# Backward convolution in descending order, Q turned ahead through scratch, weight pieces turned by one DMA each

## The chip, the cores and the metric

The kernel runs on one core of one Trainium2 chip. The metric is the device time of one execution in microseconds; three runs of the kernel before took 1823.18, 1831.09 and 1841.0 us (median 1831.09). Engines are named as in the profile: PE (TensorE), DVE (VectorE), ACT (ScalarE), POOL (GpSimd) and SP (SyncE). SP does no arithmetic; it issues DMAs, in order. Each engine works through its own instructions in order, and what another engine or a DMA has to deliver first is waited for.

## The reference, cut to what matters

One forward pass of a gated block and all its gradients: x + s * g, where s is a state-space convolution over 2048 positions and g a gated feed-forward layer. Sizes: L = 2048, D = 576, N = 128, F = 4608, all inputs bfloat16.

```python
def _fwd_reference(...):
    xn = _layernorm(A_u, axis=-1)
    # s: K[d, l] = Re sum_n C P(d, n, l) dB, P = exp(dt A l); y = conv(xn, K) + xn * Dskip
    s = _A_ref(xn, A_re, A_im, B_re, B_im, C_re, C_im, log_dt, Dskip)
    # g: silu( (silu(xn w1) * (xn w3)) w2 )
    g = _silu(_B_ref(xn, w1, w3, w2))
    return A_u + s * g

def reference(...):
    _out, _vjp = jax.vjp(_f, A_u, A_re, ..., Dskip, w1, w3, w2)
    return (_out, *_vjp(grad_out))     # the output and 12 gradients
```

## The kernel before, in words

The forward part (to about 720 us) makes the convolution kernel and its spectra, the feed-forward layer's hidden values and the output. On its way it writes to DRAM what the backward part needs: `Q_dram` (36 chunks of 128 x 2048, factors of P for 16 channels each), `PZ_dram`, the spectra `UH_dram`, `KH2_dram` and `KHz_dram`, and the hidden values `U_dram`, `G_dram`, `H_dram`.

The last stage of the forward part, `ffn_output`, makes the 16 output tiles of 128 positions. Each needs a block `hc` of H, turned by a DMA from DRAM into one of three buffers, and sums into one of three PSUM pools (psA, psB, psC, by i % 3). `finish` then computes the output and its gradients on ACT and DVE; its product `e` is the last reader of the tile's PSUM. The first loads of the backward part are issued on SP among these.

The backward part (`backward`, T0 = 700) runs 18 groups of 256 hidden columns. In each, PE makes `ph` from `w2T` and `goT`, DVE multiplies it into `gu_n` and `gg_n`, both are stored to `GU_dram` and `GG_dram` by SP, and PE makes the weight gradients from them and from `h_n` (`pgw`). `w2T` is turned by a DMA from rows of w2 in SBUF.

Beside groups 0 to 10 runs the backward convolution, in four quarters of 144 channels (`conv_bwd_quarter`). A quarter turns the incoming gradient into four spectra G (`dft_folded`), then has two halves: the first multiplies G with the spectra of u (`UH_dram`, tiles `A2`, `Az`), for i from 3 down to 0, and gives the gradient of the kernel (`gK_dram`); the second multiplies G with the kernel's spectra (`KH2_dram`, `KHz_dram`, in the same tiles) and gives the gradient of xn (`gx`, stored to `GXN_dram`). Output block i (or j) needs the spectra 0 to 3 - i, and G from i to 3. Each product is `cmul_acc`, five DVE instructions. `spectrum_variants` makes the second copy of a spectrum that `cmul_acc` reads.

From group 11 on, the gradients of the parameters are summed chunk by chunk, in 72 halves (`param_step`). `param_loads` fetches a chunk two ahead: Q's chunk, turned by a DMA from DRAM into `qT`, two pieces of `gK_dram` into `gz`, and `pz`. `param_half` then has 8 small matmuls (into `et_ps`), and DVE multiplies (`pr_q`) and sums (`S_all`).

After the groups, `phase6_inputs` makes the gradient of xn in 16 tiles: 72 steps of two matmuls each (`px`), the left side from `GG_dram` and `GU_dram`, turned by DMAs into `acts`, the right side from the turned weights w1 and w3. 26 of the 72 weight blocks (`wA`) are turned during groups 14 to 17; the other 46 come in 8 pieces of 7 or 2 blocks of 128 hidden columns, into buffers that the groups leave. `load_piece` turns a piece by five DMAs, one for each 128 (the last 64) rows of the weight. `phase5_*` finishes the parameter gradients from the sums, first turning `exp(log_dt)` into columns on PE.

What sets the order: every instruction has a priority, set by `at(us)` to a planned time, and the program is ordered per engine once, before it runs, by these and by data. `issue_after` (and `Chain`) put one instruction behind another. From group 11 on (`self.chain`), SP's DMAs keep the order of the text (`sp`). Pools with `bufs=n` make the next use of a buffer wait for the readers of the one n before. All DMA turns are issued by SP through `nat_transpose` (L1631 of the kernel before).

Of the kernel before, what the change touches and what calls it, by code (L numbers as in the profile page):

```python
# [17 lines left out]
P = 128  # L18
# [68 lines left out]
class K:  # L87
# [759 lines left out]
    def cmul_acc(self, acc, A2, Az, B, tp, first, conj):  # L847
        nc, KT = self.nc, self.cfg.KT
        Q, Wq = acc.shape[1], acc.shape[4]
        tt_ = nc.vector.tensor_tensor  # L850
        f = lambda t_: t_[:].rearrange("p q r k d -> p q r (k d)")
        if first:
            tt_(out=f(acc), in0=f(A2), in1=f(B), op=ALU.mult)
        else:
            t1 = tp.tile([P, Q, 2, KT, Wq], BF16, name="cm_t")
            tt_(out=f(t1), in0=f(A2), in1=f(B), op=ALU.mult)
            tt_(out=f(acc), in0=f(acc), in1=f(t1), op=ALU.add)
        t2 = tp.tile([P, Q, 2, KT, Wq], BF16, name="cm_t")
# [3 lines left out]
        tt_(out=f(acc)[:, :, 1], in0=f(acc)[:, :, 1], in1=f(t2)[:, :, 1], op=ALU.subtract if conj else ALU.add)  # L862

# [177 lines left out]
    def ffn_output(self, T0, TB):  # L1041
# [9 lines left out]
        with self.pool(name="o_gap", bufs=1) as gap, \  # L1051
# [38 lines left out]
            def begin(i):  # L1090
# [77 lines left out]
    def ssm_bwd_conv(self, T0, TQ, ps):  # L1168
# [3 lines left out]
        with self.pool(name="b_g", bufs=1, side="right") as self.bgp, \  # L1172
                self.pool(name="b_k", bufs=1, side="right") as kp, self.pool(name="b_z", bufs=2, side="right") as zp:
            self.at(T0)
# [52 lines left out]
    def conv_bwd_quarter(self, g, kp, zp, ps, T0, TQ):  # L1227
# [23 lines left out]
        G = []  # L1251
        first = self.pe_last
# [14 lines left out]
        if g:  # L1267
            self.at(T0)
            fold(slice(0, NB))
        for b in range(NB):  # L1270
            self.at(T0 + (TQ * 0.05 * b if g else 0))
            after = None
            if g == 0 and b == NB - 1:
# [4 lines left out]
                after = self.pe_last  # L1278
            G.append(self.bgp.tile([P, 1, 2, KT, W], BF16, name=f"g_{b}"))
            if g == 0:  # L1280
# [43 lines left out]
        for b in range(NB):  # L1324
            A2[b] = kp.tile([P, 1, 2, KT, W], BF16, name=f"a2_{b}")
            Az[b] = kp.tile([P, 1, KT, W], BF16, name=f"az_{b}")
            nc.sync.dma_start(out=A2[b][:, 0], in_=self.KH2_dram[g, b])
            nc.sync.dma_start(out=Az[b][:, 0], in_=self.KHz_dram[g, b])
        for j in range(NB):
            self.at(T0 + TQ * (0.6 + 0.1 * j))  # L1330
# [6 lines left out]
            ev = zp.tile([P, 2, W], FP32, name="gev")  # L1337
# [36 lines left out]
    def phase5_open(self, pool):  # L1374
# [3 lines left out]
        NB = self.NB  # L1378
        lr = pool.tile([NB, P], BF16, name="lg_b", tag="gh6")
        st = self.small.tile([P, 3 * NB + 3], FP32, name="sm_b")  # L1380
# [5 lines left out]
        for row, vec in self.block_rows(lr, self.aps["A_log_dt"]):  # L1386
            nc.gpsimd.dma_start(out=row, in_=vec)
        self.er = er = pool.tile([NB, P], FP32, name="er_b", tag="gh6")
        nc.scalar.activation(out=er[:], in_=lr[:], func=ACT.Exp)

    def phase5_turn(self):
        nc, NB, er = self.nc, self.NB, self.er
        pt = self.ps_T.tile([P, 512], FP32, name="et_ps")
        with self.tc.issue_after(self.pe_last.ins):
            nc.tensor.transpose(pt[:, 0:NB], er[:], self.ident_f[0:NB, 0:NB])
        nc.vector.tensor_copy(out=self.dtb[:, 0], in_=pt[:, 0:NB])
        nc.vector.tensor_tensor(out=self.dtb[:, 1], in0=self.dtb[:, 0], in1=self.dtb[:, 0], op=ALU.mult)
# [88 lines left out]
    def backward(self, T0, TG, TQ, TC, TX, gctx, mats):  # L1486
# [12 lines left out]
        with ExitStack() as out:  # L1499
# [40 lines left out]
            self.params_open(S_all, ps)  # L1540
            step = self.param_step
            hs = {}
            for gi in range(NG):
# [9 lines left out]
                for stage in group if gi == 0 else self.phase6_group(gi, cur, elp, gwp, ps_h, ps_gw):  # L1553
# [4 lines left out]
                    if stage in ("h1", "h3"):  # L1558
                        if gi < NG - 1:
                            w2(gi, stage == "h3")  # L1560
                        elif stage == "h3":
                            self.phase5_open(elp)
                        if stage == "h3" and gi + 2 < NG:
# [424 lines left out]
```

## Time and profile before

| what | us |
|---|---|
| three runs, median | 1831.09 |
| three runs, lowest and highest | 1823.18, 1841.0 |
| the profiled execution | 1837.89 |
| its span, first to last instruction | 1836.1 |
| PE busy (matmuls) | 1672.5 |
| DVE busy | 1359.4 |
| ACT busy | 912.7 |
| POOL busy | 345.2 |

The stages by the trace: forward to about 722 us; groups 0 to 10 with the backward convolution to 1206; groups 11 to 17 (parameters beside them) to 1485; the gradient of xn to the end. The groups end at 786.6, 828.2, 866.4, 908.7, 955.7, 993.1, 1039.9, 1084.4, 1125.1, 1168.7, 1205.8, 1240.5, 1277.0, 1315.2, 1353.9, 1402.8, 1439.6 and 1484.6 us.

How to read it: a line of instructions gives start, duration, engine, line of the kernel, operation, and out<-in; `x15` means that many in a row. A line of waits says who waited for whom, the total in us, how often, and the longest. SP's own instructions (SPq) are the issue of DMAs: their length is the time for which SP is held, and the data land later. All turned loads of one kind (DMA_TRANSPOSE), by the trace:

```
L1631 SPq DMA_TRANSPOSE wT<-in_B_w_dram x40: 1227/1266/3711, 1426.4 to 1530.4; - x40
L1631 SPq DMA_TRANSPOSE w2T<-w2r x36: 1200/1270/6878, 596.9 to 1380.6; - x36
L1631 SPq DMA_TRANSPOSE qT<-Q_dram x36: 1727/2520/10050, 1188.5 to 1772.2; - x36
L1631 SPq DMA_TRANSPOSE acts<-GG_dram x16: 4850/5568/13779, 1479.2 to 1782.0; - x16
L1631 SPq DMA_TRANSPOSE wA<-in_B_w_dram x10: 1425/1787/8957, 1242.9 to 1407.1; - x10
```

(least, median and longest time that one holds SP in ns, then the first and last start in us).

### The profile page before, as it was taken

What the parts mean: (1) busy time and instruction counts of PE and PEld (TensorE: products, weight loads), DVE (VectorE), ACT (ScalarE), POOL (GpSimd) and SP (SyncE); (2) the same over time, 40 slices, a digit from 0 to 9 for tenths busy, and PEclk for the clock granted to TensorE, in tenths of its full rate; (3) what the DMA queues carried; (4) which work ended last, traced back from release to release, by engine and by line L of the source; (5) the groups of instructions that cost most, each with busy time, mean ns of one, the idle gap of its engine ahead of it and who ended that gap; (6) DMA issues with size and microseconds to landing.
All of it is one profiled execution on the core that took longest, in us unless ns stands there. A gap on an engine that the chain in (4) does not pass through costs nothing. (4 is left out here: it accounts for less than half of the span.)

```text
span 1836.1 us, 38742 instructions
## 1 busy us (share of the span) xinstructions
PE 1672.5 (91%) x15573; PEld 1236.7 (67%) x15637; DVE 1359.4 (74%) x2103; ACT 912.7 (50%) x1648; POOL 345.2 (19%) x565
## 2 busy tenths in 40 slices
PE   7789999999999899799999999999979885989997
PEld 3455555554546677687788787888868774768875
DVE  7768888795864555874975979669979935867675
ACT  6778888877762112755656667554535310000101
POOL 3112222123142110011111111111111233131132
PEclk9999999999999999899999999999989997999999
DMA  7889999779799995477664656689998999999992
GB/s 223 275 270 346 316 345 313 279 262 283 236 271 231 216 212 153 167 216 207 184 196 149 197 171 190 178 254 263 229 218 221 193 224 212 217 214 232 216 254 49
DMA packets 636506, 416.91 MB, mean 227 GB/s; under 512 B 425430, under 2 KB 576966, under 8 KB 631718
## 3 DMA queue, kind: packets, MB, share of 16 engines
q1 hardware_dynamic: 580644, 287.34, 63.2%
q0 software_dynamic: 31904, 106.81, 18.1%
q10 hardware_dynamic: 23778, 20.28, 4.0%
q8 instruction: 122, 2.00, 0.5%
q14 instruction: 58, 0.48, 0.1%
HBM read 135.60 MB, written 190.89 MB: 178 GB/s over the span
## 5 line engine op out<-in xcount | busy, mean ns | idle before, releaser
L1809 PEld LDWEIGHTS <-acts 128*128 128x128 bf16 x2304 | 226.6, 99 | 84.0 <-DMA acts<-GU_dram 9.3
L1759 PEld LDWEIGHTS <-xn_bf 128*128 128x128 bf16 x2304 | 225.2, 98 | 44.1 <-issue 17.2
L1809 PE MATMUL px<-wT,acts 128*128 128x288 bf16 x1472 | 196.0, 291 | 11.5 <-DMA wT<-in_B_w_dram 11.5
L1368 DVE TENSOR_TENSOR pr_q<-et_ps,pz 128x1024 f32<-128x1024 f32 x144 | 175.9, 1221 | 31.2 <-PE et_ps L1363 23.2
L1699 PE MATMUL ph<-w2T,goT 128*128 128x256 bf16 x1440 | 177.2, 278 | 13.2 <-ACT gh L1702 9.7
L1010 PEld LDWEIGHTS <-xnT 128*128 128x128 bf16 x1152 | 107.0, 98 | 108.5 <-issue 17.5
L1371 DVE TENSOR_REDUCE S_all<-pr_q 128x32 f32<-128x1024 f32 x144 | 175.2, 1217 | 3.1
L1699 PEld LDWEIGHTS <-goT 128*128 128x128 bf16 x1440 | 142.0, 100 | 33.7 <-issue 11.3
L1010 PE MATMUL pu<-wmB_w,xnT 128*128 128x512 bf16 x568 | 152.9, 379 | 0.5 <-issue 0.2
L1739 PE MATMUL pgw<-go_o,h_n 128*128 128x288 bf16 x1152 | 150.2, 288 | 3.4 <-DVE h_n L1677 2.7
L1010 PE MATMUL pg<-wmB_w,xnT 128*128 128x512 bf16 x526 | 143.6, 379 | 7.8 <-issue 5.2
L1759 PE MATMUL pgw<-gu_n,xn_bf 128*128 128x256 bf16 x1152 | 136.7, 275 | 9.3 <-ACT gw L1743 5.2
L1739 PEld LDWEIGHTS <-h_n 128*128 128x128 bf16 x1152 | 113.2, 99 | 32.1 <-DVE h_n L1677 3.0
L1759 PE MATMUL pgw<-gg_n,xn_bf 128*128 128x256 bf16 x1152 | 130.3, 272 | 3.0 <-ACT gw L1761 2.9
L1761 ACT CAST gw<-pgw 128x256 bf16<-128x256 f32 x144 | 52.2, 374 | 146.0 <-PE pgw L1759 146.0
L1024 ACT ACTIVATE s_t<-pg 128x512 bf16<-128x512 f32 x144 | 87.8, 610 | 72.2 <-PE pu L1018 38.1
L1809 PE MATMUL px<-wA,acts 128*128 128x288 bf16 x832 | 110.6, 289 | 11.9 <-DMA acts<-GU_dram 8.7
L1702 ACT CAST gh<-ph 128x512 bf16<-128x512 f32 x144 | 82.1, 603 | 75.7 <-PE ph L1699 60.4
L660 ACT ACTIVATE cs_k<-et_ps 128x512 bf16<-128x512 int16 x216 | 111.5, 632 | 0.9 <-PE et_ps L658 0.9
L1038 POOL DMA_DIRECT2D G_dram<-g_t x72 | 52.2, 725 | 288.6 <-DVE g_t L1028 146.1
L1865 ACT ACTIVATE go<-gx 128x576 bf16<-128x576 f32 x16 | 10.9, 683 | 191.8 <-DVE gx L1848 111.5
L1029 ACT CAST u_t<-pu 128x512 bf16<-128x512 f32 x144 | 87.5, 608 | 8.4 <-PE pu L1010 7.4
(317 smaller groups left out, 3208.2 us busy)
## 6 DMA issues: line engine op xcount, KB each, us to landing
U_dram<-u_t POOLq DMA_DIRECT2D x72, 256.0 KB, 5.5
G_dram<-g_t POOLq DMA_DIRECT2D x72, 256.0 KB, 4.9
H_dram<-h_t SPq DMA_DIRECT2D x72, 256.0 KB, 3.9
Q_dram<-q_k SPq DMA_DIRECT2D x36, 512.0 KB, 5.0
h_n<-U_dram POOLq DMA_DIRECT2D x18, 1024.0 KB, 8.5
gg_n<-G_dram POOLq DMA_DIRECT2D x18, 1024.0 KB, 7.1
GU_dram<-gu_n SPq DMA_DIRECT2D x36, 512.0 KB, 4.7
GG_dram<-gg_n SPq DMA_DIRECT2D x36, 512.0 KB, 10.6
```

What stands on the lines that cost most here:

```text
L660: self.sin_last = nc.scalar.activation(out=CS[:, :, o:o + 256], in_=pt[:].bitcast(I16)[:, :, 0::2], func=ACT.Sin, scale=6.283184 / 2 ** 16)
L1010: ins = nc.tensor.matmul(pt[:], lhsT=xnT[:, c, ts], rhs=wm[w][:, c, :], start=(q == 0 and c == 0), stop=(q == 1 and c == nfull - 1))
L1024: nc.scalar.activation(out=s_t[:, :, q, :], in_=pgv, func=ACT.Silu)
L1029: nc.scalar.copy(out=u_t[:, :, q, :], in_=puv)
L1038: self.u_stores[step] = nc.gpsimd.dma_start(out=dst[fb * ng:(fb + 1) * ng, :, i0:i0 + NT, :].rearrange("g p t f -> p g (t f)"), in_=src[:] ...
L1368: nc.vector.tensor_tensor(out=pr[:].rearrange("p r k e -> p r (k e)"), in0=T[h][:].rearrange("p k z d a -> p (k z d a)")[:, None].to_broad ...
L1371: nc.vector.tensor_reduce(out=self.S_all[:, :, d0:d0 + 4], in_=pr[:].rearrange("p r k (d a) -> p (r k) d a", d=4), op=ALU.add, axis=AX.X)
L1699: self.pe_last = nc.tensor.matmul(ph[j][:, k, :].rearrange("p (a f) -> p a f", f=P), lhsT=lw, rhs=rh, start=(n == 0), stop=(n == nfull))
L1702: self.sc(lambda: nc.scalar.copy(out=gh[:, j], in_=ph[j][:]))
L1739: self.pe_last = nc.tensor.matmul(pgw[pi_][:, 0:pw], lhsT=hn[:, tt, fl * P:(fl + 1) * P], rhs=go_o[:, tt, po:po + pw], start=(tt == 0), st ...
L1759: self.pe_last = nc.tensor.matmul(pw_[:, 0:FG], lhsT=self.xn_bf[:, tt, c * P:(c + 1) * P], rhs=nat[:, tt, :], start=(tt == 0), stop=(tt == ...
L1809: self.pe_last = nc.tensor.matmul(px[pi_][:, 0:pw], lhsT=acts[i][:, ai, fi, :], rhs=w[:, po:po + pw], start=(n == 0), stop=(n == len(steps ...
```

## The change

1. **Q turned ahead.** `turn_q(n, after)` turns n chunks, each in two halves: a DMA turn of 128 x 1024 into one of two buffers, and a plain store of it to a new scratch `QT_dram`. All are chained on SP: turn 0, turn 1, store 0, turn 2, store 1, and so on. It is called in the backward convolution, behind the spectra's loads: 3 chunks beside the second half of quarter 0, 3 and 3 beside quarters 1 and 2, 3 and 6 beside quarter 3: 24. The next half's spectra are loaded behind the last store (`q_last`). `param_loads` then fetches chunks 0 to 23 by one plain DMA of 512 KB; chunks 24 to 35 are turned as before.
2. **Descending second halves.** The second half runs j from 3 to 0, and its last block takes its products in the order 0, 3, 1, 2. In quarters 1 to 3, G is made from 3 down to 0, the first half is planned from 0.1 of the quarter, and `spectrum_variants` is made for one spectrum at a time, just ahead of its first use. `gx` and its partner `gev` move from a pool of two buffers to one of one.
3. **One DMA per weight piece** in `load_piece`: 576 rows at once.
4. **log_dt.** `phase5_open` is called ahead of the groups, and not in the last one; the vector is turned on PE as it is, and the exponential is taken by ACT from PSUM afterwards.
5. **At the end of the forward part**: the last output tile sums in psC instead of psA; the rows of w2 are first loaded behind hc 7 (was 4), and the first turns of w2T stand behind hc 13.

```diff
@@ ffn_output
-                return i, hc, x_t, go_t, s_t, (psA, psB, psC)[i % 3].tile([P, 2, 512], FP32, name="po")
+                return i, hc, x_t, go_t, s_t, (psA, psB, psC)[i % 3 if i < LT - 1 else 2].tile([P, 2, 512], FP32, name="po")
@@ ssm_bwd_conv
+            self.turnp, self.turned_q, self.q_last = turnp, 0, None
+            self.QT_dram = self.dram.tile([cfg.D // 16, P, 16 * cfg.N], BF16, name="QT_dram")
@@ conv_bwd_quarter, first half
-            with self.tc.issue_after(self.hc_loads[2 * b + 4].ins) if g == 0 else nullcontext():
-                nc.sync.dma_start(out=A2[b][:, 0, 0], in_=self.UH_dram[g, b, :, 0])
-                nc.sync.dma_start(out=Az[b][:, 0], in_=self.UH_dram[g, b, :, 1])
-            with self.tc.issue_after(self.epi[2 * b + 7].ins) if g == 0 else nullcontext():
-                self.spectrum_variants(A2[b], Az[b])
+            sync = Chain(self.tc, nc.sync)
+            sync.prev = (ld if b else self.q_last) if g else self.hc_loads[2 * b + 4]
+            sync.dma_start(out=A2[b][:, 0, 0], in_=self.UH_dram[g, b, :, 0])
+            ld = sync.dma_start(out=Az[b][:, 0], in_=self.UH_dram[g, b, :, 1])
+            if g == 0:
+                with self.tc.issue_after(self.epi[2 * b + 7].ins):
+                    self.spectrum_variants(A2[b], Az[b])
+        self.at(T0 + TQ * 0.1)
+        self.turn_q(3 if g else 0, ld)
...
-        for b in range(NB):
-            self.at(T0 + (TQ * 0.05 * b if g else 0))
+        for b in range(NB - 1, -1, -1) if g else range(NB):
+            self.at(T0 + (TQ * 0.05 * (NB - 1 - b) if g else 0))
...
         for i in range(NB - 1, -1, -1):
-            self.at(T0 + TQ * (0.2 + 0.1 * (NB - 1 - i)))
+            self.at(T0 + TQ * ((0.1 if g else 0.2) + 0.1 * (NB - 1 - i)))
+            if g:
+                b = NB - 1 - i
+                with self.tc.issue_after(self.cm_last.ins) if b else nullcontext():
+                    self.spectrum_variants(A2[b], Az[b])
@@ conv_bwd_quarter, second half
+            sync.prev = ld if b else self.q_last
+            sync.dma_start(out=A2[b][:, 0], in_=self.KH2_dram[g, b])
+            ld = sync.dma_start(out=Az[b][:, 0], in_=self.KHz_dram[g, b])
+        self.turn_q(3 if g < 3 else 6, ld)
-        for j in range(NB):
+        for j in range(NB - 1, -1, -1):
...
-            for k, i in enumerate(range(NB - j)):
+            for k, i in enumerate(range(NB - j) if j else (0, 3, 1, 2)):
...
-            gx = zp.tile([P, KT, W], FP32, name="gx")
+            gx = self.gxp.tile([P, KT, W], FP32, name="gx")
@@ new
+    def turn_q(self, n, after):
+        nc, cfg = self.nc, self.cfg
+        put = None
+        for k in range(2 * n):
+            ch, h = divmod(k, 2)
+            ch += self.turned_q
+            cols = slice(h * 8 * cfg.N, (h + 1) * 8 * cfg.N)
+            t = self.turnp.tile([P, 8, cfg.N], BF16, name="q_s")
+            with self.tc.issue_after(after.ins):
+                after = nc.sync.dma_start_transpose(out=t[:], in_=self.Q_dram[ch][:, cols])
+            if put is not None:
+                with self.tc.issue_after(after.ins):
+                    after = nc.sync.dma_start(out=put[0], in_=put[1])
+            put = self.QT_dram[ch][:, cols], t[:].rearrange("p k n -> p (k n)")
+        if n:
+            with self.tc.issue_after(after.ins):
+                after = nc.sync.dma_start(out=put[0], in_=put[1])
+        self.turned_q += n
+        self.q_last = after
@@ param_loads
-        self.nat_transpose(qT[:], self.Q_dram[ch])
+        if ch < self.turned_q:
+            self.sp(lambda: nc.sync.dma_start(out=qT[:].rearrange("p k n -> p (k n)"), in_=self.QT_dram[ch]))
+        else:
+            self.nat_transpose(qT[:], self.Q_dram[ch])
@@ phase5_open, phase5_turn
-        self.er = er = pool.tile([NB, P], FP32, name="er_b", tag="gh6")
-        nc.scalar.activation(out=er[:], in_=lr[:], func=ACT.Exp)
...
-            nc.tensor.transpose(pt[:, 0:NB], er[:], self.ident_f[0:NB, 0:NB])
-        nc.vector.tensor_copy(out=self.dtb[:, 0], in_=pt[:, 0:NB])
+            nc.tensor.transpose(pt, self.lr[:], self.ident_bf[0:NB, 0:NB])
+        nc.scalar.activation(out=self.dtb[:, 0], in_=pt, func=ACT.Exp)
@@ backward
-            with self.tc.issue_after(self.hc_loads[4].ins):
+            with self.tc.issue_after(self.hc_loads[7].ins):
                 self.w2row_load(0)
...
             step = self.param_step
+            self.phase5_open(elp)
@@ load_piece
-        for c in range(self.cfg.DT):
-            self.load_wT_rows(wT[-1], c)
+        self.nat_transpose(t[:], self.aps[("B_w1", "B_w3")[ai]][:, f0 * P:(f0 + n) * P])
@@ phase6_load_w2
-            self.nat_transpose(w2T[:, fl], self.w2rows[gi % 2][:, fl])
+            with self.tc.issue_after(self.hc_loads[13].ins) if gi == 0 else nullcontext():
+                self.nat_transpose(w2T[:, fl], self.w2rows[gi % 2][:, fl])
```

More of the change, by code (lines that the diff above doesn't have):

```diff
@@ L861, in cmul_acc @@
         tt_(out=f(acc)[:, :, 0], in0=f(acc)[:, :, 0], in1=f(t2)[:, :, 0], op=ALU.add if conj else ALU.subtract)
-        tt_(out=f(acc)[:, :, 1], in0=f(acc)[:, :, 1], in1=f(t2)[:, :, 1], op=ALU.subtract if conj else ALU.add)
+        self.cm_last = tt_(out=f(acc)[:, :, 1], in0=f(acc)[:, :, 1], in1=f(t2)[:, :, 1],
+                           op=ALU.subtract if conj else ALU.add)
     def ssm_conv(self, T0, TC, ps, ps1):
@@ L1172, in ssm_bwd_conv @@
         with self.pool(name="b_g", bufs=1, side="right") as self.bgp, \
[L1173 removed]
+                self.pool(name="b_k", bufs=1, side="right") as kp, self.pool(name="b_z", bufs=2, side="right") as zp, \
+                self.pool(name="b_x", bufs=1, side="right") as self.gxp, self.pool(name="b_q", bufs=2, side="right") as turnp:
             self.at(T0)
@@ L1278, in conv_bwd_quarter @@
                 after = self.pe_last
-            G.append(self.bgp.tile([P, 1, 2, KT, W], BF16, name=f"g_{b}"))
+            G[b] = self.bgp.tile([P, 1, 2, KT, W], BF16, name=f"g_{b}")
             if g == 0:
@@ L1326, in conv_bwd_quarter @@
             Az[b] = kp.tile([P, 1, KT, W], BF16, name=f"az_{b}")
-            nc.sync.dma_start(out=A2[b][:, 0], in_=self.KH2_dram[g, b])
-            nc.sync.dma_start(out=Az[b][:, 0], in_=self.KHz_dram[g, b])
-        for j in range(NB):
-            self.at(T0 + TQ * (0.6 + 0.1 * j))
+            sync = Chain(self.tc, nc.sync)
+            sync.prev = ld if b else self.q_last
[3 more added lines that the diff above has]
+        for j in range(NB - 1, -1, -1):
+            self.at(T0 + TQ * (0.6 + 0.1 * (NB - 1 - j)))
             Z = zp.tile([P, 1, 2, KT, W], BF16, name="Z")
-            for k, i in enumerate(range(NB - j)):
+            for k, i in enumerate(range(NB - j) if j else (0, 3, 1, 2)):
                 self.cmul_acc(Z, A2[i], Az[i], G[i + j], zp, k == 0, True)
-            gx = zp.tile([P, KT, W], FP32, name="gx")
+            gx = self.gxp.tile([P, KT, W], FP32, name="gx")
             even = self.idft_side(ps.tile([P, 512], FP32, name="et_ps"), Z, 0, 0, 2)
             odd = self.idft_side(ps.tile([P, 512], FP32, name="et_ps"), Z, 1, 0, 2).rearrange("p (k d) -> p k d", k=2)
-            ev = zp.tile([P, 2, W], FP32, name="gev")
+            ev = self.gxp.tile([P, 2, W], FP32, name="gev")
             nc.scalar.copy(out=ev[:].rearrange("p k d -> p (k d)"), in_=even)
@@ L1378, in phase5_open @@
         NB = self.NB
-        lr = pool.tile([NB, P], BF16, name="lg_b", tag="gh6")
+        self.lr = lr = self.small.tile([NB, P], BF16, name="lg_r")
         st = self.small.tile([P, 3 * NB + 3], FP32, name="sm_b")
@@ L1386, in phase5_open @@
         for row, vec in self.block_rows(lr, self.aps["A_log_dt"]):
-            nc.gpsimd.dma_start(out=row, in_=vec)
-        self.er = er = pool.tile([NB, P], FP32, name="er_b", tag="gh6")
-        nc.scalar.activation(out=er[:], in_=lr[:], func=ACT.Exp)
+            self.gp(lambda: nc.gpsimd.dma_start(out=row, in_=vec))
     def phase5_turn(self):
-        nc, NB, er = self.nc, self.NB, self.er
-        pt = self.ps_T.tile([P, 512], FP32, name="et_ps")
+        nc, NB = self.nc, self.NB
+        pt = self.ps_T.tile([P, 512], FP32, name="et_ps")[:].bitcast(BF16)[:, 0:NB]
         with self.tc.issue_after(self.pe_last.ins):
-            nc.tensor.transpose(pt[:, 0:NB], er[:], self.ident_f[0:NB, 0:NB])
-        nc.vector.tensor_copy(out=self.dtb[:, 0], in_=pt[:, 0:NB])
+            nc.tensor.transpose(pt, self.lr[:], self.ident_bf[0:NB, 0:NB])
+        nc.scalar.activation(out=self.dtb[:, 0], in_=pt, func=ACT.Exp)
         nc.vector.tensor_tensor(out=self.dtb[:, 1], in0=self.dtb[:, 0], in1=self.dtb[:, 0], op=ALU.mult)
@@ L1560, in backward @@
                             w2(gi, stage == "h3")
-                        elif stage == "h3":
-                            self.phase5_open(elp)
                         if stage == "h3" and gi + 2 < NG:
```

2 lines of the change are left out of this document (1 added, 1 removed).

## The prediction

> **What bounds the kernel now.** I read the table of stretches first, to find where TensorE (PE) is not full.
>
> ```profile
> 1200.00:1300.00 100.00, 97.03 (x950) 83.55 (x948) 84.11 (x91) 51.03 (x85) 13.59 (x23) 1.00 0.98 244
> 1300.00:1400.00 100.00, 85.40 (x817) 73.06 (x816) 87.52 (x95) 45.02 (x73) 10.34 (x17) 0.95 0.98 232
> 1400.00:1500.00 100.00, 88.17 (x834) 74.52 (x832) 82.30 (x104) 31.20 (x58) 22.23 (x40) 0.97 0.93 211
> 1500.00:1600.00 100.00, 80.89 (x651) 62.15 (x649) 58.61 (x76) 8.22 (x16) 28.08 (x53) 0.90 1.07 215
> 1700.00:1800.00 100.00, 99.36 (x856) 80.28 (x855) 70.37 (x91) 10.21 (x19) 23.21 (x42) 1.00 1.16 232
> ```
>
> The columns are the stretch, then busy us of PE, weight loads, VectorE (DVE), ScalarE and GpSimd, then PE's clock, DMA share and GB/s. PE is the bound (97 to 99%) except from 1300 to 1640, where its clock sinks as well. The list of PE's waits says why:
>
> ```profile
> PE et_ps L1363 <- DMA gz<-gK_dram: 17.0, 3, 9.8
> ...
> PE px L1809 <- DMA wT<-in_B_w_dram: 11.5, 5, 4.4
> ...
> PE px L1809 <- DMA acts<-GU_dram: 8.7, 2, 7.2
> PE po L1110 <- DMA hcC<-H_dram: 8.0, 2, 5.0
> ...
> PE et_ps L1395 <- ACT er_b L1389: 4.6, 1, 4.6
> ...
> PE ph L1699 <- DVE e L1122: 3.6, 1, 3.6
> PE px L1809 <- DMA acts<-GG_dram: 3.3, 1, 3.3
> ```
>
> Nearly all are loads that Sync (SP) issues. SP's timeline shows that it is late, since its own instructions are long:
>
> ```profile
> 1440.66 4.20 SPq L1631 DMA_TRANSPOSE qT<-Q_dram  x1
> ...
> 1446.94 20.69 SPq L1631 DMA_TRANSPOSE wT<-in_B_w_dram  x15
> ...
> 1472.93 3.45 SPq L1722 DMA_DIRECT2D GG_dram<-gg_n  x2
> 1479.25 6.04 SPq L1631 DMA_TRANSPOSE acts<-GG_dram  x1
> ...
> 1501.87 29.84 SPq L1631 DMA_TRANSPOSE wT<-in_B_w_dram  x20
> ```
>
> A turning DMA holds SP until its descriptors are out; a plain one, like pz, takes 0.53 us. The `gg_n` that is stored at 1472.93 was ready at 1449.4 (last product, L1717, in the chain of waits): 23 us lost in SP's queue. From 1190 to 1470 SP's instructions sum to 241 of 280 us, 73 of them 19 turns of Q (3.8 each).
>
> **The change, part by part**, in times of the profiled execution.
>
> *Q from scratch.* The last turn of the 24 chunks replaces a load of 3.8 us on SP by one of about 0.5 (pz, 0.53). Chunks 0 to 19 are those loaded before 1470: 19 x 3.3 = 63 us of SP go from 1190-1470, so SP is no longer behind. The wait for gz at 1354.2 (9.8 us) was this lag: the chunk's turn was issued at 1351.46, its gz at 1356.06. The group of that wait lasted 1353.9 to 1402.8 (49.0 us), the group before 38.7. What is late next is VectorE: 40.1 us of it per group (sum of durations, which overlap a little) in a 38.7 us group, so I do not go below 38.7. Gain 10.3.
>
> *log_dt early, exponential after the turn.* PE no longer waits at 1459.3 (4.6 us), and the slow clock behind it goes in part, since DVE's parameter products (1.2 us each, back to back in the chain from 1464.8) follow closely: gain 6, of at most 7.5.
>
> *One DMA per weight piece.* 8 pieces, 40 DMAs to 8. The merged form (576 rows at once) is in no row. Bounds: the five parts (7 blocks of 128x128 in 1.27 us, so 6.3 for a piece of 31.5 blocks) and the least row per block (wA, 15 blocks in 1.43, so 3.0). I take the rate of `acts`, 36 blocks in 5.57: 0.155 x 31.5 = 4.9 us, and for the two small pieces (9 blocks) 1.4. The x15 become 4.9 + 4.9 + 1.4 = 11.2 (from 20.7), the x20 become 16.1 (from 29.8).
> The Trainium skill ("DMA: Bandwidth & Descriptors", Latency and other measured facts) gives 261 GB/s for a DMA transpose; acts has 1.18 MB in 5.57 us = 212 GB/s. By the page a piece takes 3.95 us, and the sum below would grow by about 2.
>
> *SP replayed from group 17 on, on PE's old clock.* The x15 may start when the buffers are free (PE leaves gg_n and gu_n at about 1440), end at 1452; one parameter load (0.5 + 1.2 + 0.5 = 2.3) to 1454; four stores (4.5) to 1458.5, landed at 1463 (6.3 after the first GG issue, as before). Acts for two tiles: 4 x 5.5 to 1485; the first GG half lands near 1473, before PE is free at 1478.6 (1484.6 - 6). So the waits of 3.3 and 1.4 at px go: gain 4.7. The x20 end at 1502, landed by 1507; PE needs those pieces after two times 49 steps (98 x 0.245 = 24) and 2 x 9 steps, at about 1507. The third tile's GG half may be issued when tile 0 has passed step 65 (about 1509) and lands 9.9 later (row's median) at 1519; PE stands from 1514.5: 4.5 us stay. Two parameter loads (4.6 instead of the 11.7 between 1536.7 and 1548.4) and the GU half: 1.5 more stay. Second half of tile 2 starts at about 1531 instead of 1558.5: 27 gained, of which 10.7 are counted, so 16 here. Behind it go the rest of 1586-1640: 1.4, the gz wait of 6.1 at 1615 and its slow clock (60 matmuls in 9.63 instead of 7.35): 9.8.
>
> *w2T's first turns behind hc 13.* Before, three w2T turns (4.29 us at 596.9) stand ahead of an hcC at 601.28, and PE stood 5.0 at 606.5, then ran 32 matmuls in 6.44 instead of 4.08, then stood 0.95: gain 8.3. They now stand where SP idles about 4 us per tile (677.9 to 683.0), with PE needing the next hc 19 us later. If that cover were gone, the same 8 would come back.
>
> *Last output tile in psC.* ph no longer waits for the freed psA (3.56); the tile now waits for tile 14's `e`, which comes 4.3 after its products, covered by 21 ph matmuls (2.4): gain 1.7.
>
> *Turning 24 chunks in the backward convolution (785 to 1200).* 48 half turns and 48 stores, each store ahead of the turn after next. Two buffers: turn k+2 waits until store k has landed, so a half costs landing + one turn. Turn: 1.27 (w2T, 5 blocks; 8 blocks lie next to it). Landing of a 256 KB store: 2.5 (E_dram) to 6.0 (PZ_dram); I take 3.5, near H_dram's 3.9, since this stage's DMA share is 0.5 to 0.7 against 0.8 to 0.97 for H's. So 4.8 per half, bounds 3.8 and 7.3. Queued behind on SP: convolution loads, w2T and the GU/GG stores. SP is busy 146 of the 405 us there, so 259 / 48 = 5.4 us per half are free. w2T has a whole group of slack (two buffers). The convolution's loads have little: they are now chained behind the turns. DVE waits 16.4 us for them before (12.2 and 4.2), which descending order, asking for one new block per step, can take away; and DVE has 28% free there. Cost between -6 (part of those waits reaches PE) and 22 (7 half quarters x 4.4 landing, less 9 that DVE's slack takes); I take 8. The last twelve halves (58, with 9 of other work) end near 1198, and the first parameter product is at 1213: loads land at 1207, 6 us of cover; if it is gone, up to 5 on PE.
>
> *Without cost:* the descending loop has the same products; the single gx buffer makes DVE wait at most some 2 us per quarter (8 DVE instructions, 5 us, against the 6.2 landing).
>
> Sum: 10.3 + 6 + 4.7 + 16 + 9.8 + 8.3 + 1.7 - 8 = 48.8. The profiled run took 1837.9 (span 1836.1), so 1789; it was 0.4% above the median of the three, so about 1783 as a median.
>
> **Rivals.** (1) Slower: SP overflows in the convolution. At 6.4 us per half (landing 5.1) the lag is 48 x 6.4 - 259 = 48 and eats the gain; at 7.3 (PZ's landing) it is 91: 1831 - 57 + 91 = 1865. For it: GS_dram and gK_dram stores land in 4.5 and 5.0 in this very stage. Against: the last quarter's lag falls behind the convolution, and DVE's slack takes part. Chance 0.13.
> The Trainium skill (same page, Anatomy of one DMA) warns that the completion write can be surprisingly late where the target is HBM, which is this rival's cause; no row here splits a landing.
> (2) The DMA engines, not SP's issue, set the weight pieces: share 1.07 at 1500. Then pieces take what their parts took (3.39 MB in 29.84 us, 114 GB/s); against it, acts moves 212 GB/s beside them. 9.5 + 13.7 less on SP, nearly all on the path: 48.8 - 23 = 26, so 1805; with bounds 1798 to 1818. Chance 0.17.
> (3) The chained loads are exposed once per half quarter: 7 x 5 = 35 on PE in place of my 8. 1810 to 1830, at 1822 near no change. Against: five of every ten products need no new block. Chance 0.10.
> Forecast as summed, 1765 to 1800: 0.60.
>
> **Numbers.** About 1% (18 us) can be told from no change. Faster: 0.60 + two thirds of (2) = 0.71; same: the rest of (2) and (3) = 0.16; slower: 0.13. The range: low end, both unknown prices at their good ends (-6 for turning, pieces at 3.0) 1831 - 63 = 1768, less 2 for the skipped slow clock: 1766; high end 1831, which takes in (2) and (3) and leaves (1) out.
>
> **What would show it.** Right: no gz wait above 1 us; wT rows x8 near 4.9 us; group 14 near 38 us; SP's GG store of group 17 within 10 us of its product; PE at 95% or more from 1500 to 1600; no wait for hcC near 606. Wrong: QT stores landing above 5 us, waits of DVE for the a and az loads, PE waits at L827 and L837 larger than the 14 us in all now; a merged piece above 6 us; groups 13 to 16 longer than 39 us, with DVE full.

## The result

The changed kernel is no faster: 1851.32 us in the median of its runs against 1841.0 for the kernel before on the same chip, a ratio of 1.0097 (95% interval 1.007 to 1.0124). The forecast was 1783. Its profiled execution took 1843.97 us (span 1842.2), that of the kernel before 1837.89. A few executions of each kernel are longer, at a lower granted clock (here 1887.34 us at 0.966, where most have 0.970 to 0.976); the ratios leave these out.

Three times of each trace say where it went: the end of the forward part, the last weight gradient of group 10 (the convolution lies beside groups 0 to 10), and the end.

| | forward ends | group 10 ends | forward to group 10 | group 10 to the end | profiled execution |
|---|---|---|---|---|---|
| before | 721.8 | 1205.8 | 484.0 | 632.1 | 1837.89 |
| after | 722.6 | 1248.8 | 526.2 | 595.2 | 1843.97 |

So 37 us were won behind the convolution, where 46.8 were forecast, and 42 were lost beside it. The table of stretches shows both, first two rows of the kernel before, then the changed kernel (stretch, its length, busy us of PE, weight loads, DVE, ACT and POOL, PE's clock, DMA share, GB/s):

```profile
850.00:950.00 100.00, 94.24 (x935) 82.28 (x934) 80.73 (x143) 64.26 (x115) 11.40 (x19) 0.98 0.65 191
950.00:1050.00 100.00, 93.90 (x963) 81.38 (x961) 69.14 (x130) 61.03 (x114) 11.98 (x20) 1.00 0.60 184
```

```profile
850.00:950.00 100.00, 88.73 (x886) 77.74 (x884) 72.39 (x137) 61.47 (x111) 10.64 (x18) 0.95 0.89 233
950.00:1050.00 100.00, 80.91 (x787) 69.47 (x785) 65.72 (x125) 50.87 (x96) 9.57 (x16) 0.93 0.90 199
...
1350.00:1450.00 100.00, 95.31 (x936) 81.74 (x934) 98.55 (x107) 45.59 (x77) 13.31 (x22) 1.00 0.92 252
```

PE, busy 94.24 and 93.90 us in the first two stretches before, is now busy 88.73 and 80.91. DVE is less busy there too, so neither arithmetic engine is the bound: both wait. Around 1400 it is the reverse: PE 95 at full clock, DVE 98.6, no wait for gz. The changed kernel's list of waits from 800 to 1290 says for what (who, for whom, us in all, times, longest):

```profile
DVE gx L1354 <- DMA GXN_dram<-gx: 25.8, 4, 8.6
PE et_ps L837 <- DVE Z L861: 16.0, 3, 9.4
PE et_ps L827 <- DVE ZZ L1314: 14.7, 5, 10.2
...
DVE gm L1272 <- DMA gs<-GS_dram: 11.6, 1, 11.6
ACT g L818 <- DMA q_s<-Q_dram: 9.0, 1, 9.0
PE et_ps L816 <- ACT g L818: 8.1, 1, 8.1
DVE a L843 <- DMA a<-UH_dram: 7.5, 1, 7.5
```

PE waits for the inverse transforms' inputs (ZZ, Z) and for ACT; these in turn wait for DMAs: the store of the one gx buffer, loads (gs, a) that SP issues, and, on ACT, a turn of Q. The DMA engines are fuller (share 0.89 and 0.90 instead of 0.65 and 0.60), but that alone does not make these DMAs land later: from 800 to 1200, from issue to landing, `a` of UH takes 4.7 us (median) in both kernels, gs 3.7 instead of 5.2, the store of gx 3.9 instead of 6.2 (though GU's stores take 7.8 instead of 4.3). What is late is the issue of the loads. SP's timeline around the latest of them:

```profile
989.59 1.25 SPq L1367 DMA_TRANSPOSE q_s<-Q_dram  x1
990.94 0.52 SPq L1370 DMA_DIRECT2D QT_dram<-q_s  x1
991.56 2.76 SPq L1665 DMA_TRANSPOSE w2T<-w2r  x2
994.47 6.33 SPq L1367 DMA_TRANSPOSE q_s<-Q_dram  x1
1000.84 0.93 SPq L1370 DMA_DIRECT2D QT_dram<-q_s  x1
1001.81 2.50 SPq L1757 DMA_DIRECT2D GU_dram<-gu_n  x2
1004.41 5.16 SPq L1757 DMA_DIRECT2D GG_dram<-gg_n  x2
1009.66 3.78 SPq L1367 DMA_TRANSPOSE q_s<-Q_dram  x1
...
1022.88 0.33 SPq L1374 DMA_DIRECT2D QT_dram<-q_s  x1
1023.30 0.38 SPq L1245 DMA_DIRECT2D gs<-GS_dram  x1
```

The last of six halves is stored at 1022.88, and only then is gs of the next quarter loaded (995.98 in the kernel before). DVE's timeline shows what that does, since the fold of gs stands among the products of the running quarter:

```profile
1015.07 0.45 DVE L862 TENSOR_TENSOR Z<-Z,cm_t 128x576 bf16<-128x576 bf16 x1
1027.12 0.76 DVE L1272 TENSOR_TENSOR gm<-gs 128x1152 bf16<-128x1152 bf16 x1 [11.60 <-DMA gs<-GS_dram]
1027.79 0.75 DVE L857 TENSOR_TENSOR Z<-Z,cm_t 128x1152 bf16<-128x1152 bf16 x1
```

For 11.6 us DVE has a product at hand and cannot reach it. PE's longest wait for ZZ (10.2, at 1033) is this one.

The chains of six halves, by SP's timeline from the first turn to the last store:

| begins | 805.0 | 867.0 | 920.5 | 979.4 | 1046.6 | 1111.5 | 1160.6 (12 halves) |
|---|---|---|---|---|---|---|---|
| lasts, us | 47.7 | 29.0 | 49.4 | 43.8 | 45.6 | 29.0 | 70.5 |
| other DMAs on SP within | 16 | 3 | 11 | 8 | 11 | 0 | 11 |

Alone or nearly so, a half takes 4.8 us, the figure that was forecast. With other DMAs between (GU, GG, w2T, gK) it takes 7.3 to 8.2 in four chains, and 5.9 in the chain of twelve.

The price is not spread over the chains. Against the kernel without turns (e1 below), group by group, the changed kernel loses 10.0 us in group 3, 11.9 in group 6 and 4.8 in group 7; in each other group up to 10 it is 2.0 or less. Group 6 is the wait for gs above. In group 7 DVE waits 8.6 us for the store of gx, and PE 9.4 behind it. In group 3 ACT is held:

```profile
868.01 0.70 ACT L818 CAST g<-et_ps 128x288 bf16<-128x288 f32 x2
877.31 0.37 ACTq L1356 DMA_DIRECT2D GXN_dram<-gx  x1
877.71 6.26 ACT L818 CAST g<-et_ps 128x288 bf16<-128x288 f32 x14 [9.01 <-DMA q_s<-Q_dram]
```

ACT cannot issue its store of gx until a turn of Q has landed (why is told in the last section), and `g`, which PE needs, stands behind it. PE's wait of 8.1 us at 878 is its only one above 0.5 in this group.

### The profile page after: what moved, and what is told of

Same layout as the page of the kernel before. It is cut to its first block, busy times and chain, and to the rows that moved or that the text cites. A ratio compares the mean times of both kernels' runs of the same rounds, so it can differ in the third digit from the quotient of the medians.

```text
span 1842.2 us, 38838 instructions
## 1 busy us (share of the span) xinstructions
PE 1671.9 (91%) x15573; PEld 1240.0 (67%) x15637; DVE 1360.2 (74%) x2102; ACT 912.8 (50%) x1648; POOL 346.0 (19%) x565
## 5 line engine op out<-in xcount | busy, mean ns | idle before, releaser
L1406 DVE TENSOR_TENSOR pr_q<-et_ps,pz 128x1024 f32<-128x1024 f32 x144 | 175.8, 1221 | 21.8 <-PE et_ps L1401 8.8
L1844 PE MATMUL px<-wT,acts 128*128 128x288 bf16 x1472 | 189.7, 286 | 0.4 <-DMA wT<-in_B_w_dram 0.4
L1844 PE MATMUL px<-wA,acts 128*128 128x288 bf16 x832 | 111.4, 290 | 10.3 <-DMA acts<-GU_dram 7.4
## 6 DMA issues: line engine op xcount, KB each, us to landing
GG_dram<-gg_n SPq DMA_DIRECT2D x36, 512.0 KB, 10.7
```

Source lines behind the costliest of these rows:

```text
L1406: nc.vector.tensor_tensor(out=pr[:].rearrange("p r k e -> p r (k e)"), in0=T[h][:].rearrange("p k z d a -> p (k z d a)")[:, None].to_broad ...
L1844: self.pe_last = nc.tensor.matmul(px[pi_][:, 0:pw], lhsT=acts[i][:, ai, fi, :], rhs=w[:, po:po + pw], start=(n == 0), stop=(n == len(steps ...
```

## The experiments

Two theories, and they add: **W** (L in the later expectations), that chains of turns delay what stands behind them on SP or hold ACT, and **X**, that the single gx buffer costs by itself. Rivals: the descending order (D), a fixed price per turned chunk (P), the number of DMAs rather than bytes (N). The column from forward to group 10 is the measure; it takes out the forward part, which ended between 714 and 730 in these profiles.

| run | ratio to before, 95% | forward to group 10 | group 10 to the end |
|---|---|---|---|
| e1 no turns, gx single | 0.9986 (0.995 to 1.0021) | 495.3 | 619.9 |
| e2 no turns, gx twofold | 0.9872 (0.9804 to 0.994) | 474.5 | 623.3 |
| e3 outer edits alone | 0.993 (0.9886 to 0.9974) | 484.8 | 617.0 |
| e4 GXN stored by POOL | 1.0175 (1.0111 to 1.024) | 535.3 | 608.3 |
| e5 gs loaded earlier | 1.0138 (1.0094 to 1.0183) | 531.8 | 606.8 |
| e6 gx twofold, quarter turns | 1.0618 (1.0535 to 1.0701) | 599.6 | 618.6 |
| e7 e5 and e6 | 1.0566 (1.0493 to 1.0639) | 587.7 | 626.0 |
| e8 16 chunks instead of 24 | 0.9979 (0.993 to 1.0028) | 506.0 | 600.1 |
| e9 GU, GG stored by POOL | 1.0091 (1.0046 to 1.0137) | 524.1 | 603.2 |
| e10 e2 in ascending order | 0.9888 (0.9814 to 0.9962) | 481.7 | 622.5 |
| e11 9 chunks, gx twofold | 0.9898 (0.9832 to 0.9965) | 477.8 | 620.6 |
| e12 9 late chunks, gx twofold | 0.9872 (0.9811 to 0.9934) | 477.0 | 606.4 |
| e13 e1 in ascending order | 1.0 (0.9948 to 1.0052) | 494.2 | 636.6 |

**e1, e2: no turns in the convolution, with one gx buffer and with two.**

```diff
-        self.turn_q(3 if g else 0, ld)
+        self.turn_q(0, ld)
...
-        self.turn_q(3 if g < 3 else 6, ld)
+        self.turn_q(0, ld)
# e2 also
-                self.pool(name="b_x", bufs=1, side="right") as self.gxp, ...
+                self.pool(name="b_x", bufs=2, side="right") as self.gxp, ...
```

> The changed kernel without its turns of Q in the convolution: all 36 chunks are turned by their parameter loads again, as before; descending order, chained loads, one gx buffer, merged weight pieces and the rest stay. Theory W (the turns delay loads and hold ACT in its order, and that is what groups 3 to 10 lost): group 10 ends within 10 us of the 1205.8 of the kernel before instead of 1248.8; the gz waits of groups 15 and 17 come back (about 15); execution 1844 - 40 + 15 = about 1819 (1810 to 1828). Rival X (the single gx buffer costs, whatever else runs): group 10 still ends at 1230 or later, DVE's waits for GXN stay near 19 us, execution 1840 to 1860. Rival D (the descending order and the variants made inside the loop cost): group 10 at 1230 or later without those waits for GXN.

> As the kernel without turns, and gx and gev have two buffers again (the room that the halves of Q took is free). Theory W: group 10 ends within 4 us of where it ends in the kernel without turns, execution within 5 us of it. Rival X: group 10 ends 10 us or more earlier than with one buffer, no later than 1212. Rival D: both end at 1230 or later.

Both theories hold, each for a part. Without turns the stage falls from 526.2 to 495.3 (group 10 ends at 1215.9: 30.9 from the turns); with the second buffer to 474.5 (1193.3: 20.8 from the buffer). D is out: with two buffers the descending order is shorter than before. The total of e1 was missed (1835.8, expected 1819), since a group 11 of 44.4 us instead of 34.7 took 10 of it back. This is the price of turning Q at its old place: a parameter load's turn of a whole chunk held SP for 14.24 us from 1203.22, GG of group 10 was stored behind it at 1218.82, POOL could load gg_n into the same buffer at 1227.99, and ACT waited 8.2 us for that. So the shares are taken at the end of group 10. One profile each carries them, but the groups that an edit leaves alone repeat well: in groups 1, 3, 4, 6, 8 and 9 the two runs differ by 0.2 us or less.

e1 has one buffer for gev too, which was not tested alone; but e11 and e12 below have two for gx and one for gev, and lose 0.5 us at most in groups 5, 7 and 10, where one gx costs 18.2 (in group 2 they lose 3.6 and 0.7, so its 3.4 may be gev's).

What one buffer does is seen on DVE at the same place of e2 (first fence) and of e1 (second):

```profile
1155.28 0.46 DVE L1354 TENSOR_TENSOR gx<-gev,et_ps 128x288 f32<-128x288 f32 x1 [7.59 <-PE et_ps L837]
1155.65 0.45 DVE L1355 TENSOR_TENSOR gx<-gev,et_ps 128x288 f32<-128x288 f32 x1
1156.02 0.75 DVE L853 TENSOR_TENSOR Z<-a,g 128x1152 bf16<-128x1152 bf16 x1
1156.69 0.45 DVE L1354 TENSOR_TENSOR gx<-gev,et_ps 128x288 f32<-128x288 f32 x1
```

```profile
1172.51 0.45 DVE L1355 TENSOR_TENSOR gx<-gev,et_ps 128x288 f32<-128x288 f32 x1
...
1179.89 0.45 DVE L1354 TENSOR_TENSOR gx<-gev,et_ps 128x288 f32<-128x288 f32 x1 [3.94 <-DMA GXN_dram<-gx]
```

With two buffers the next gx follows after one DVE instruction, 1.0 us later: the last two matmuls of one block (L837) had stood behind the group's products on PE, and the next block's sixteen follow them at once (18 in a row at 1154.88). With one buffer, five DVE instructions that are ready run first, and then it waits for the store to land (7.2 us at the median in e2). Behind it on DVE stand the products of the next block, and PE waits 4.89 us for them at 1187.8; behind the store on ACT, which issues it, `gh` waits 5.30. Groups 2, 5, 7 and 10, where a quarter ends, are 3.4, 6.2, 6.2 and 5.7 us longer: 21.5.

**e3: the edits outside the convolution alone** (parts 3, 4 and 5 of the change, on the kernel before).

> The kernel before with only the edits outside the convolution: merged weight pieces, log_dt loaded early, w2T behind a later load, the last forward tile's PSUM. Theory: groups 0 to 17 end as in the kernel before (group 17 near 1484, with the gz waits), and the stage of px after them is as short as in the changed kernel (318 from its first product instead of 339.6): 1837.9 - 21 = about 1817 (1808 to 1824). Rival (the stage was short only because the convolution's delay or the earlier turns left SP free ahead of it): 1830 or more.

Confirmed in size: 1819.6, ratio 0.993. But it is not the stage of px alone: from group 10 to the end 15.1 us are won, of them 5.2 in group 17 (39.8 instead of 45.0, no wait for er_b). The other 21.8 of the 36.9 that the changed kernel won there go with the turned chunks: it and e1, which differ in the turns alone, are 24.7 apart there.

**e4: the store of gx by POOL.**

```diff
-            nc.scalar.dma_start(out=self.GXN_dram[:, j * KT:(j + 1) * KT, cs], in_=gx[:])
+            nc.gpsimd.dma_start(out=self.GXN_dram[:, j * KT:(j + 1) * KT, cs], in_=gx[:])
```

> The changed kernel with the store of gx to GXN issued by POOL instead of ACT. If ACT held in its order behind that store (for the lane of its DMA that a turn still had, or for gx) is a large part of the loss: ACT's wait for q_s (9.0) and its late gh and gw behind gx (23.7 and 9.0) go, group 10 ends 15 to 25 us earlier (1224 to 1234) and the execution takes 1820 to 1830. If the loss is in the loads behind the turns or in DVE's wait for the single gx: group 10 within 6 us of 1248.8, execution 1838 to 1848.

A miss on both sides: 9 us longer. ACT's wait for q_s is gone, but POOL now stands 60.0 us before these stores waiting for gx, and DVE's waits for gs rose to 38.1 (longest 23.8). So ACT's place in the matter was not shown by this run: POOL, which carries the store in order, is held by it instead, and group 3 alone takes 71.3 us (54.2 in the changed kernel).

**e5, e6, e7: gs earlier; two gx buffers with quarter turns; both.**

```diff
# e5: behind the first half's turns, ahead of the KH2 loads
+        if g < 3:
+            self.gs_next = kp.tile([P, LT, W], BF16, name="gs")
+            with self.tc.issue_after(self.q_last.ins):
+                self.q_last = nc.sync.dma_start(out=self.gs_next[:], in_=self.GS_dram[g + 1])
# e6: room for two gx (and one gev) by smaller buffers for Q
-        for k in range(2 * n):
-            ch, h = divmod(k, 2)
+        for k in range(4 * n):
+            ch, h = divmod(k, 4)
-            t = self.turnp.tile([P, 8, cfg.N], BF16, name="q_s")
+            t = self.turnp.tile([P, 4, cfg.N], BF16, name="q_s")
```

> The changed kernel with the load of gs for the next quarter issued in the middle of the quarter, ahead of the second turns and of the KH2 and KHz loads, instead of behind them. Theory L (loads that stand behind turns on SP are a good part of what turning costs): DVE's wait of gm for gs (16.7 in all, longest 11.6) falls under 4, PE's waits of the inverse transforms for ZZ (21.8) by some 10, group 10 ends at 1236 to 1242 instead of 1248.8 and the execution takes 1834 to 1839. Rival (the single gx holds DVE there anyway, so that an earlier gs only waits elsewhere): group 10 within 4 us of 1248.8, execution 1840 to 1848.

> The changed kernel, all its turns kept, with two buffers for gx again; the room comes from turning quarters of a chunk (128x4x128) instead of halves, so twice as many turns and stores of half the size. Theory X (what the single gx costs, 22 us at group 10 between the two kernels without turns, is paid here too): group 10 ends near 1227 (1221 to 1233), execution 1818 to 1826. Rival N (the gx cost does not add to the turns, or the number of DMAs is what costs): group 10 at 1240 or later, execution 1838 or more.

> Both edits: two gx buffers with quarter turns, and gs loaded in the middle of the quarter. If both theories hold and add: group 10 near 1217 (1210 to 1223), execution 1808 to 1816. If gs early gains nothing by itself: as with two buffers alone. If the number of DMAs costs: 1235 or more.

e5 settles nothing, by its own making: the load still stands behind the first half's chain and is issued at 1019.86 instead of 1023.30, so the longest wait for gs is 10.7 instead of 11.6, while ACT's wait for a turn of Q grew from 9.0 to 12.1. e6 went far the other way, and that is its worth. Against e2, which has no turns, the same bytes in twice as many DMAs cost 125 us (599.6 to 474.5), although gx has two buffers; in halves they cost 30.9. Its waits from 800 to 1390:

```profile
DVE a L843 <- DMA a<-UH_dram: 56.5, 2, 32.5
...
PE et_ps L827 <- DVE ZZ L1314: 44.0, 3, 16.1
...
ACT g L818 <- DMA az<-UH_dram: 17.5, 1, 17.5
DVE gm L1272 <- DMA gs<-GS_dram: 17.5, 1, 17.5
...
PE et_ps L837 <- DVE Z L861: 4.7, 2, 4.0
```

The waits for gx's store are gone; most is lost on loads behind the chains, which now last 47 to 82 us for a half quarter, and some on ACT, which waits 18.7 us for turns of Q. A turn of half the size holds SP nearly as long (1.20 us median, 1.35 for a half) and lands in 3.6 instead of 4.6; its store lands in 2.5 instead of 2.9. The Trainium skill ("DMA: Bandwidth & Descriptors", Anatomy of one DMA — SWDGE (gpsimd) path) gives a DMA that GpSimd issues a fixed cost of about 2.0 us, which does not grow with its size. The two store landings agree, though SP issues them: 128 KB more take 0.4 us more, which leaves an estimated 2.1 us that the size does not touch. e7 (587.7) says the same as e6: the number of DMAs costs.

**e8: 16 chunks instead of 24** (2 per half quarter, 4 in the last).

> The changed kernel with two chunks turned per half quarter instead of three (four instead of six in the last; 16 in all, the rest by their parameter loads). Theory L (what costs is the length of a chain of turns: loads behind it come late once it is longer than the half quarter can spare): chains of some 30 us instead of 44 to 50, the waits of DVE for a and gs (7.5 and 11.6) nearly gone; group 10 ends at 1216 to 1226, execution 1815 to 1833. Rival P (each turned chunk costs the same, 33 us for 24 between this kernel and the one without turns): group 10 at 1236 to 1240, execution near 1838.

W against P, and P falls: 506.0, group 10 at 1226.5. The waits from 800 to 1290:

```profile
DVE gx L1354 <- DMA GXN_dram<-gx: 22.0, 4, 7.3
...
PE et_ps L837 <- DVE Z L861: 17.8, 3, 8.1
...
PE et_ps L827 <- DVE ZZ L1314: 2.2, 4, 1.1
...
DVE gm L1272 <- DMA gs<-GS_dram: 1.4, 1, 1.4
```

Late loads are gone (1.4 us are left of 11.6, a's 7.5 wholly), and so is ACT's wait for a turn of Q; gx's share is not. The first 16 chunks cost 10.7 us (0.7 each), the next 8 cost 20.2 (2.5 each). Of these 20.2, 11.4 are in group 6 and 6.7 in group 3. So the price of the last eight is mainly two waits that come or do not come, one for a load behind a chain and one of ACT for a turn. At which length of chain they set in was not tested.

**e9: the stores of GU and GG by POOL** for groups 0 to 10.

```diff
-                self.sp(lambda: nc.sync.dma_start(out=dst[ts, ...
+                self.sp(lambda: (nc.sync if gi > 10 else nc.gpsimd).dma_start(out=dst[ts, ...
```

> The changed kernel with the stores of GU and GG of groups 0 to 10 issued by POOL instead of SP. If the chains of turns last 44 to 50 us instead of 29 because these stores stand among them and hold SP (2.5 and 5.2 us in one chain, and waits for DVE): chains of 30 to 38 us, group 10 ends at 1232 to 1240, execution 1826 to 1836. Rival: the chain is as long by the turns' and stores' landings alone, or POOL's queue now delays the groups' own loads: group 10 at 1246 or later, execution 1842 or more.

The rival, nearly: 2 us shorter in the stage. The chains in the busy half quarters still last 39 to 43 us (one 61), and the quiet ones 33 instead of 29. SP's timeline says where the time goes. In the four slow chains of six halves of the changed kernel, other DMAs hold SP for 11 to 24 us, and it stands idle between the links for 10 to 15. In e9's chains of 39 to 43 us other DMAs hold it for 5 to 10 only, but it stands idle for 18 to 21: stores of Q land in 4.2 us there (median; 2.9 in the changed kernel). Why they land later was not tested.

**e10, e13: ascending second halves**, without turns, with two gx buffers and with one.

> The kernel without turns and with two gx buffers, its second halves in ascending order again. If the descending order is what made groups 0 to 11 10 us shorter than in the kernel with the outer edits alone (1227.0 instead of 1237.4): group 11 ends near 1237, execution near 1822. If that came from elsewhere (chained loads, variants in the loop): group 11 within 4 us of 1227, execution 1809 to 1816.

> The kernel without turns, second halves in ascending order, with the single gx buffer: is what one buffer costs a matter of the order? If it costs because the halves with one and with two products come back to back in either order: group 10 ends 15 to 25 us after the 1197.3 of the same order with two buffers. If it is the descending order that brings the first two gx together: within 8 us of 1197.3.

Descending is 7 us shorter to group 10 and loses 0.8 behind it. The whole profiles are only 3.2 apart, since e2's forward part, which has no edit between the two, took 3.2 longer; the ratios, 0.9872 and 0.9888, are not told apart. One buffer costs in this order as well. The profiled execution of e13 is a long one (1854.6; median 1830.5), so its 12.5 us more to group 10 are not used, and the ratios must serve: 1.0 (0.9948 to 1.0052) against 0.9888 (0.9814 to 0.9962), 1.1% or 20 us, with these intervals around it. So the buffer has a price in either order; that it is the same price is not shown.

**e11, e12: nine chunks turned, gx twofold.** One buffer for a half of Q, each turn behind the store before; one chunk per half quarter and three in the last. e11 turns chunks 0 to 8, e12 18 to 26.

```diff
-            self.turnp, self.turned_q, self.q_last = turnp, 0, None
+            self.turnp, self.turned_q, self.q_last = turnp, 18, None
...
-        if ch < self.turned_q:
+        if 18 <= ch < self.turned_q:
```

> A candidate: two gx buffers, one gev, one buffer for halves of Q, one chunk turned per half quarter and three in the last (9 chunks; each turn waits for the store before). Theory L: a chain of two halves in series is about 17 us and hides: group 10 ends within 6 us of the 1193.3 without turns, the gz waits of groups 15 and 16 and of the px stage (1.2, 6.4, 6.8) go, execution 1800 to 1812. Rival P: 9 x 1.4 = 12 later, group 10 near 1206, execution 1815 to 1822.

> As the candidate with one chunk per half quarter, but the nine chunks turned in the convolution are 18 to 26, which are loaded while px runs, instead of 0 to 8. If SP's work around the start of px is what PE waits for there (gz 14.6 in the px stage of the candidate): the stage of px falls from 343.6 to about 325, groups 15 and 16 are as without turns (39.3 and 43.1): 1813.6 + 8 - 18 = execution near 1805 (1798 to 1811). If those waits only move on (to acts and to the weight pieces): 1812 or more.

Nine chunks in chains this short cost 2.5 to 3.3 us (474.5 to 477.8 and 477.0). In e11 groups 14 to 17 lose nothing (38.1, 38.1, 36.7, 39.8), yet the end does not come: PE's waits for gz after 1230 are 14.6 us in both e2 and e11, moved into the stage of px. In e12 they are 3.5:

```profile
PE px L1838 <- DMA acts<-GU_dram: 11.3, 4, 6.2
...
PE et_ps L1395 <- DMA gz<-gK_dram: 3.5, 2, 3.2
...
PE px L1838 <- DMA acts<-GG_dram: 2.6, 1, 2.6
```

Group 10 to the end takes 606.4 instead of 620.6. e12 is the best profile here (1804.57), as expected; by ratio it and e2 are 1.3% below the kernel before (0.9872 each), and e2, e11 and e12 are not told apart.

## Why the prediction was wrong, step by step

The forecast of the profiled execution was 1789 and it took 1843.97, 55 us more: 34 beside the convolution (42 lost instead of 8), 10 behind it (36.9 won instead of 46.8) and 11 in the forward part (0.8 lost instead of 10 won). The 42 us between 484.0 and 526.2 divide by runs: outer edits 0.8 (e3), descending order with its loads and variants -10.3 (e2 against e3; by e10, 7.2 of it are the order), single gx buffer 20.8 (e1), 16 chunks turned 10.7 (e8), eight more 20.2.

- **"The single gx buffer makes DVE wait at most some 2 us per quarter": failed.** It was put under "without cost" and had no term in the sum. It costs 20.8 us, 5.2 a quarter. The step took eight DVE instructions between two gx; the trace has one, since PE, held up by the group's products, ends one block and makes the next at once. And it followed the wait on DVE alone, not to the products queued behind it, nor to ACT behind the store. The kernel before gave a sign: with two buffers DVE already waited for these stores.

```profile
DVE gx L1339 <- DMA GXN_dram<-gx: 9.4, 3, 5.4
```

- **Turning Q in the convolution, 8 us (bounds -6 to 22): failed**, at 30.9. 4.8 us per half came out for a chain alone (29.0 for six), but partly by luck: the sum was the store's landing (3.5) and one turn (1.27), while the store landed in 2.9 (median) and had to wait first for its turn to land (4.6), which the sum left out; with two halves under way the last turns of the chain at 1111.5 follow each other every 4.0 to 4.5 us, and its start takes the rest. The budget of 5.4 was a mean over the stage: the groups' DMAs fall into the same stretches, and there a half takes 7.3 to 8.2 and the chain 44 to 50 us. SP overflows there, as in rival (1), but not by its cause, landings of 5.1 us and more. Rival (3) comes nearest in price (35 on PE), not in kind: it had a late load in each of seven half quarters, while 26.7 of the 30.9 lie in three groups, one with a late load (gs), one with ACT held behind a turn, one with the store of gx. That a turn could hold ACT was in no term and no rival. "DVE's slack takes part" was wrong where a late load's instruction stands in DVE's order ahead of work that is ready.
- **The sum behind the convolution, 46.8: mechanism right, size 36.9.** The wait for gz at 1354 is gone, and groups 13 to 16 take 38.2, 38.1, 38.1 and 36.7 with DVE full, close to the "not below 38.7". The merged piece, estimated at 4.9, measured (least, median, longest, in ns):

```profile
L1665 SPq DMA_TRANSPOSE wT<-in_B_w_dram x8: 1306/4844/7639, 1459.0 to 1537.2; - x8
```

  The four pieces behind the first tiles' acts took 17.00 us together (16.1 forecast, 29.84 in parts before), so rival (2) falls; only the first piece, at 7.64, passed the 6 us named as a sign of being wrong. GG of group 17, finished at 1489.0, is stored at 1490.87 instead of 23 us late. PE waits 0.4 us for wT (11.5 before). What stays is acts: 7.4 and 2.9, where 4.5 and 1.5 were left in the sum; PE is busy 88.3% from 1500 to 1600, not the 95% that was to show the forecast right.
- **er_b: 6 forecast, 5.2 measured** (group 17 in e3).
- **The forward edits, 10: hardly seen.** PE's wait for hcC fell from 8.0 to 3.1, and from the first output tile (568.6 and 573.9) to the last 4.4 us were won; but the forward part ends at 722.6, against 721.8: the execution was 5.3 late before any edit. The other runs all have these edits. Over the 14 profiles with them, nine take 147.2 to 149.5 us from the first output tile to the last, with 2.9 to 3.5 of waiting for hcC, and five take 152.2 to 155.2, with 5.7 to 9.5; the one profile without them has 153.5 and 8.0. So some 5 of the 10 us are won in most executions and none in the others; what decides it stays open.

The range missed because turning was bounded at 22 and the single buffer left at nothing; they cost 31 and 21, and add. (The range's low end, 1831 - 63, holds the 14 us of the turning alone, and not the pieces at 3.0; that changes nothing here.)

## What to carry to other kernels

A chain of DMAs on an in-order issuer is to be sized against the busiest stretch it passes through, with all that the engine issues there, and its end compared with the next load behind it: with 16 chunks the waits for late loads were 1.4 us, with 24 they were 11.6 and 7.5. Halving a buffer to make room is a cost of its own: look in the trace how closely two uses follow, and who else stands behind the waiting instruction on every engine involved. Work that is moved ahead is best chosen by where its relief lands: in one profile each, nine late chunks gained at the end what nine early ones only moved on (606.4 against 620.6 us).

## What the runs showed of the hardware

ACT waited 9.0 us for the landing of q_s, which it never reads: it issues gx's store, and in the program that store waits for a completion semaphore that DMAs of SP and of ACT use by turns. The trace's records show this: eight semaphores serve the DMAs of both, the store issued at 877.31 waits for the one that it will count on itself, and that one's last DMA was the turn of Q issued at 868.44. So a slow chain on SP can hold ACT, and PE behind it (8.1 us at 878); in e5 ACT waited 12.1 us so, in e6 18.7 in two waits, in e8 not at all. And PE's clock sinks with its waits: 0.93 from 950 to 1050, where it was 1.00 before.
